# Query projections on 64 rows each, token splits read from PSUM, and MLP products placed among the last attention turns

## The chip, the core and the metric

The kernel runs on one core of a Trainium2 chip. The metric is the device time of one execution in microseconds. Engines are named as in the profile: PE is TensorE, PEld its weight loads, DVE is VectorE, ACT is ScalarE, POOL is GpSimd and SP is SyncE. PSUM has eight banks of 512 fp32 columns over 128 partitions.

## The reference

Linear attention with a positive feature map over 4 batches, 8 heads, 576 tokens and head size 64, then two MLPs of width 2048 on 2304 tokens of 512 features.

```python
def phi(x):
    proj = np.einsum('bhsd,df->bhsf', x, w_phi)
    proj = proj - np.max(np.abs(proj), axis=-1, keepdims=True)
    return np.concatenate([np.exp(proj), np.exp(-proj)], axis=-1)
q_p, k_p = phi(q), phi(k)
kv = np.einsum('bhsf,bhsd->bhfd', k_p, v);  z = np.sum(k_p, axis=2)
x = einsum(q_p, kv) / (einsum(q_p, z) + 1e-6)      # tokens x 512
h = x @ w1_in;  g = max(0.01 * h, h);          x = g @ w1_out
h = x @ w2_in;  g = h * tanh(softplus(h));     out = g @ w2_out
```

## The kernel before

**Precision.** A matmul whose operands are marked F32R is one pass of a shortened format. To keep accuracy each operand is split into a high part (an ACT copy) and a low part (a DVE subtraction), `split` at lines 79 to 81, and each product is three matmuls, `three` at lines 83 to 86: high by high, high by low, low by high. Plain fp32 matmuls (the attention's sums) go to the array as two instructions each, so that the trace counts 64 where the program writes 32.

**Attention.** The work goes by pairs of heads: 16 pairs, four to a batch. `attention(n)`, line 515, is one turn for n from 0 to 16. It works on five pairs at once: it loads n+3, transposes pair n+2, projects pair n+1 (`q_proj`, `k_proj`), takes the exponentials and the key-value sums of pair n (`k_exp`, `kv`, `kv_copy`), the output sums of pair n-1 (`nd`), and normalises pair n-2 and transposes it to features by tokens (`normalise`, `x_left`, `x_t`). Nothing reorders this: every engine runs its instructions in the order in which the code issues them. An odd n has one more key group to project and guard (`k_proj_left`); an even n has one more transpose to split.

**Query projection before.** A transposed query tile has 128 partitions: rows 0 to 63 are the features of an even token, rows 64 to 127 those of an odd one. The weights `wbh`, `wbl` are block diagonal (`wbd`, lines 253 to 258): the 128 columns of half `o` are zero in the rows of the other half. `q_proj(i, c)`, line 391, runs for c = 0 to 3 (head h, half o): three matmuls on all 128 rows with 256 or 320 columns into one bank of the ring "a" (four banks), then an ACT copy of the bank to `qd` (line 403). After both halves of a head, POOL takes the maximum over partitions (line 408), and `q_guard` (line 412, DVE) subtracts it.

**Weight conversion beside it.** The weights of the MLPs arrive as 64-bit words and are converted on DVE and ACT, one piece in each turn from 1 to 15 (`conv0`): lines 134 and 136 at the turn's begin, an ACT scale (150), and two DVE steps (159, 162) near its end. The ten first pieces are split in the following turn: ACT line 215, then DVE line 216, ahead of `normalise` in DVE's order.

**Tokens to MLP.** `x_t` ends with two ACT copies into `X`: 64 left-over columns (line 485, from the bank that `nd` writes, `outs`) and 512 columns from the bank `xt` (line 487). `window(0, (p,))`, called after turns 8 to 11 (line 781), splits one 128-row piece of batch 0's tokens from `X` into the MLP's operands, lines 80 and 81. `moe(0)` and `moe(1)` stand at the ends of turns 15 and 16. Each emits one product of the first MLP (`emit_h`, 12 matmuls of 512 columns) and its activation (`leaky`). After the turns the last `x_t(15)` follows, the attention's banks (`outs`, `kvp`, `xt`) are released and become the ring "b", and `moe(2)`, `moe(3)`, ... run the MLPs: each emits a product h and, two steps later, the output product of an earlier one.

Of the kernel before, what the change touches and what calls it, by code (L numbers as in the profile page):

```python
# [23 lines left out]
def attention_two_mlps_kernel(  # L24
# [12 lines left out]
    nc = tc.nc  # L37
# [38 lines left out]
    def bank(ring):  # L76
        return rings[ring].tile([P, 512], F32, tag=ring, name=ring)

    def split(hi, lo, src):
        nc.scalar.activation(out=hi, in_=src, func=AF.Copy)  # L80
        nc.vector.tensor_tensor(out=lo, in0=src, in1=hi.bitcast(F32), op=ALU.subtract)

    def three(o, wh_, wl_, xh, xl, start=True, stop=True):
        nc.tensor.matmul(out=o, lhsT=wh_, rhs=xh, start=start, stop=False)  # L84
        nc.tensor.matmul(out=o, lhsT=wh_, rhs=xl, start=False, stop=False)  # L85
        nc.tensor.matmul(out=o, lhsT=wl_, rhs=xh, start=False, stop=stop)  # L86
# [164 lines left out]
    with tc.manual_schedule():  # L251
# [136 lines left out]
            nc.scalar.activation(out=e, in_=src, func=AF.Exp, scale=float(sg))  # L388
            return e

        def q_proj(i, c):
            s = st[i]
            h, o = divmod(c, 2)
            if "qd" not in s:
                s["qd"] = ap.tile([P, 2, S], F32, tag="qd", name="qd")
                s["qm"] = ap.tile([P, 2, S], F32, tag="qm", name="qm", bufs=1)
            t = bank("a")
            n = HM + (h == o) * LEFT
            c0 = h * (HM + (1 - o) * LEFT)
            d0 = (1 - o) * (HM + h * LEFT)  # L400
            f = slice(o * F, (o + 1) * F)
            three(t[:, 0:n], wbh[:, f], wbl[:, f], s["qh"][:, c0:c0 + n], s["ql"][:, c0:c0 + n])
            nc.scalar.activation(out=s["qd"][:, h, d0:d0 + n], in_=t[:, 0:n], func=AF.Copy)  # L403
            half = s.setdefault("half", set())
            half.add(c)
            if {2 * h, 2 * h + 1} <= half:
                qd, qm = s["qd"][:, h, :], s["qm"][:, h, :]
                nc.gpsimd.partition_all_reduce(qm, qd, P, bass_isa.ReduceOp.absmax)  # L408

        def q_guard(i):  # L410
            s = st[i]
# [65 lines left out]
        def x_t(i):  # L477
            s = st[i]
            b, p = divmod(i, NP)
            t = pa.tile([P, 512], F32, tag="xt", name="xt")  # L480
            for j in range(NM):
                nc.tensor.transpose(out=t[:, j * P:(j + 1) * P], in_=s["xn"][:, j].rearrange("p h d -> p (h d)"), identity=ident)
            o = s["nd"][:, 1, MAIN - LEFT:MAIN]
            nc.tensor.matmul(out=o, lhsT=s["xl"].rearrange("p h d -> p (h d)"), rhs=fold, start=True, stop=True)
            nc.scalar.activation(out=X[:, p, C0 + b * LEFT:C0 + (b + 1) * LEFT], in_=o, func=AF.Copy)
            st[i] = None
            return lambda: nc.scalar.activation(out=X[:, p, b * MAIN:(b + 1) * MAIN], in_=t, func=AF.Copy)

        def k_exp(i, a):
# [5 lines left out]
        def start():  # L495

            transposes(0, "k")
            split(wbh, wbl, wbd.rearrange("p a f -> p (a f)"))
            transposes(0, "q")
            k_proj(0, 0)  # L500
            transposes(0, "l")
            q_left(0)
            q_proj(0, 1)
            q_proj(0, 2)
            k_proj(0, 1)
            q_proj(0, 0)
            q_proj(0, 3)
            k_proj_left(0)
            transposes(1, "q", "k")
            q_left(1)  # L510
            q_guard(0)
            load(2)
            conv0.load(1)

        def attention(n):

            x, o, w, p, t = (i if 0 <= i < PAIRS else None for i in range(n - 2, n + 3))
            x_copy = lambda: None  # L520
            if n + 3 < PAIRS:
                load(n + 3)
            if t is not None and t > 1:
                values(t)
            if n >= CONV0:
                conv0.begin()
                conv0.split()
            if p is not None:
                for c in range(4):
                    q_proj(p, c)  # L530
            if x is not None and n < PAIRS:
                normalise(x)
                x_left(x)
            if p is not None:
                for c in range(2):
                    k_proj(p, c)
                if p % 2 == 0:
                    k_proj_left(p)
            if w is not None:
                k_exp(w, 0)  # L540
            if x is not None:
                x_copy = x_t(x)
            if t is not None:
                transposes(t)
                q_left(t)
            if w is not None:
                k_exp(w, 1)
            x_copy()
            conv0.scale()
            if o is not None:  # L550
                nd(o)
            if p is not None:
                q_guard(p)
            conv0.join()
            if w is not None:
                st[w]["qp"] = [exp(st[w]["qd"], "qp", sg) for sg in (1, -1)]
                for a in range(2):
                    kv(w, a)
                kv_copy(w)
            if p is None:  # L560
                normalise(o)
                x_left(o)
            if p is None:
                moe(n - PAIRS + 1)

        order = [(0, MAIN), (MAIN, MAIN), (C0, B * LEFT)] + [(j * MAIN, MAIN) for j in range(2, B)]
        blocks = [(a, c0, n) for a in range(2) for c0, n in order]
        NB = len(blocks)
        win = {}

        def window(j, chunks=range(KD)):
            a, c0, n = blocks[j]
            for kk in chunks:
                hi = winp.tile([P, MAIN], F32R, tag="wh", name="wh")[:, 0:n]
                lo = winp.tile([P, MAIN], F32R, tag="wl", name="wl")[:, 0:n]
                split(hi, lo, X[:, kk, c0:c0 + n])
                win.setdefault(j, []).append((hi, lo))


# [138 lines left out]
        def moe(g):  # L718
            for x in [g, g + 1] if g == jump else [g + 1] if g > jump else [g]:
                if x < len(seq):  # L720
                    emit_h(seq[x])
                    if seq[x][1][-1] == M - 1 and seq[x][0] + 1 < NB:
                        window(seq[x][0] + 1)
            if g < len(seq):
                j, ms = seq[g]
                if j <= last1:
                    between = leaky(seq[g])
                    if j == 0 and ms[0] >= HEAD:
                        conv1.step(*between)
                        if not conv1.done():  # L730
                            conv1.step()
                        if conv1.at == len(conv1.units):
                            conv2.load(1)
                    else:
                        for f in between:
                            f()
            if 0 <= g - 2 < len(seq) and seq[g - 2][0] <= last1:
                j, ms = seq[g - 2]
                emit_o(seq[g - 2])
                if ms[-1] == M - 1:  # L740
                    for d in range(KD):
                        finish(j, d)
                if 0 < j < last1:
                    conv2.step()
                    if conv2.done() and not w_st:
                        load_w2(0)
                if j == last1:
                    m = ms[0]
                    split_w2(m, (0, 1) if m < M - 1 else (0,))
                    if m < M - 1:  # L750
                        load_w2(m + 1, (0, 1) if m < M - 2 else (0,))
                    else:
                        load_w2(m, (1,))
                        tail[0] = g + 1
            if g == tail[0]:
                split_w2(M - 1, (1,))
            done = None
            if 0 <= g - 3 < len(seq) and seq[g - 3][0] > last1:
                j, ms = seq[g - 3]
                if seq[g - 3] == seq[-1]:  # L760

                    emit_o(seq[-1], (0, 1))
                    finish(j, 0)
                    finish(j, 1)
                    for d in (2, 3):
                        for it in seq[-2:]:
                            emit_o(it, (d,))
                        finish(j, d)
                elif seq[g - 3] == seq[-2]:
                    emit_o(seq[-2], (0, 1))  # L770
                else:
                    emit_o(seq[g - 3])
                    if ms[-1] == M - 1:
                        done = j
            mish(g, done)

        start()
        for n in range(PAIRS + 1):
            attention(n)
            if 0 <= n - PAIRS // 2 < KD:  # L780
                window(0, (n - PAIRS // 2,))
        x_t(PAIRS - 1)()
        ap.release()
        pa.release()
# [44 lines left out]
```

## Time and profile before

| what | value |
|---|---|
| median of 3 runs | 981.86 us (980.54 to 982.08) |
| profiled execution | 982.12 us, of which the span of its instructions is 980.0 us |
| PE busy | 957.1 us (98%), mean granted clock 0.996 |
| DVE busy | 715.9 us (73%) |
| ACT busy | 507.2 us (52%) |
| POOL busy | 69.0 us (7%) |

The busy shares are means over two stages: some 190 us of attention, and the MLPs after them. The slices of the page show PE at 8 or 9 tenths in the attention and at 9 in nearly all that follows; DVE is at 8 and 9 in the attention. Which wait ends last has to be read in each stage for itself.

### The profile page before, as it was taken

Reading aid. Unit: us, or ns where it says so; the run is one execution under the profiler, and the core shown is the slowest. Engines: PE = TensorE matmul, PEld = TensorE weight load, DVE = VectorE, ACT = ScalarE, POOL = GpSimd, SP = SyncE. Lnnn points to the kernel's source line nnn. Section 1 sums busy time; section 2 is a strip of 40 time slices with the busy share of each in tenths; the row PEclk is TensorE's granted clock in tenths of the full one; section 3 lists DMA queues with packets and bytes.
Section 4 is the critical chain, followed back from the end, with each engine's and each line's share of the span. In section 5 each row is a group of like instructions: output and inputs, shape, how many; then the busy total and the mean of one; then the engine's idle time right before and its main releaser. Section 6 shows DMA issues by size and latency. Waiting matters only on the chain.

```text
span 980.0 us, 16741 instructions
## 1 busy us (share of the span) xinstructions
PE 957.1 (98%) x6704; PEld 818.4 (84%) x6704; DVE 715.9 (73%) x1271; ACT 507.2 (52%) x886; POOL 69.0 (7%) x36
## 2 busy tenths in 40 slices
PE   7999889899999999999999999999999999999998
PEld 7999778788888889988888888888888988888886
DVE  7899889389936665765334459878977788778875
ACT  5899879555523333333333456445545455445543
POOL 3443434000000000000000000000000000000000
PEclk9999999999999999999999999999999999999999
DMA  7444543235404444442203310001000100001001
GB/s 200 123 130 136 141 112 108 77 115 161 134 22 143 148 142 148 131 147 100 76 1 112 104 55 11 1 1 43 1 1 1 43 1 23 1 0 43 1 1 43
DMA packets 68205, 72.97 MB, mean 74 GB/s; under 512 B 27168, under 2 KB 52640, under 8 KB 68128
## 3 DMA queue, kind: packets, MB, share of 16 engines
q1 hardware_dynamic: 67392, 71.52, 23.8%
q8 instruction: 52, 0.85, 0.4%
q10 hardware_dynamic: 736, 0.39, 0.1%
q14 instruction: 25, 0.20, 0.1%
HBM read 57.48 MB, written 14.42 MB: 73 GB/s over the span
## 4 chain that ended last, share of the span: by engine, by line
PE 83%; DVE 7%; ACT 7%; issue 1%; DMA 0%; POOL 0%; POOLq 0%; ACTq 0%; DVEq 0%
PE a L84 14%; PE a L85 14%; PE a L86 14%; PE b L86 13%; PE b L85 13%; PE b L84 13%; ACT kp L388 2%; ACT qp L388 1%; DVE wl L216 1%; DVE xn L464 1%; DVE mx L365 1%; PE outs L448 1%; DVE qd L412 1%; DVE kd L366 1%; ACT xleft L474 1%
## 5 line engine op out<-in xcount | busy, mean ns | idle before, releaser
L84 PE MATMUL a<-wh,wh 128*128 128x512 f32 (+1 forms) x640 | 235.7, 368 | 0.0
L86 PE MATMUL a<-wh,wl 128*128 128x512 f32 (+1 forms) x640 | 235.4, 368 | 0.0
L85 PE MATMUL a<-wl,wh 128*128 128x512 f32 (+1 forms) x640 | 235.4, 368 | 0.0
L84 PEld LDWEIGHTS a<-wh,wh 128*128 128x128 f32 x640 | 120.6, 188 | 20.4 <-issue 0.2
L85 PEld LDWEIGHTS a<-wl,wh 128*128 128x128 f32 x640 | 120.7, 189 | 20.3
L86 PEld LDWEIGHTS a<-wh,wl 128*128 128x128 f32 x640 | 120.6, 188 | 19.9
L661 DVE TENSOR_TENSOR gl<-g,gh 128x512 fp32r<-128x512 f32 x72 | 49.8, 692 | 110.2 <-ACT gh L658 110.2
L85 PE MATMUL b<-gl,wh 128*128 128x512 f32 (+1 forms) x320 | 117.7, 368 | 0.0
L84 PE MATMUL b<-gh,wh 128*128 128x512 f32 (+1 forms) x320 | 117.7, 368 | 0.0
L86 PE MATMUL b<-gh,wl 128*128 128x512 f32 (+1 forms) x320 | 117.7, 368 | 0.0
L86 PE MATMUL b<-wh,gl 128*128 128x512 f32 x288 | 112.2, 390 | 0.0
L85 PE MATMUL b<-wl,gh 128*128 128x512 f32 x288 | 112.2, 389 | 0.0
L84 PE MATMUL b<-wh,gh 128*128 128x512 f32 x288 | 112.1, 389 | 0.0
L658 ACT ACTIVATE gh<-g 128x512 fp32r<-128x512 f32 x72 | 45.5, 632 | 116.0 <-PE b L86 110.7
L683 ACT ACTIVATE gh<-u 128x512 fp32r<-128x512 f32 x72 | 45.5, 633 | 70.3 <-PE b L85 63.6
L657 DVE TENSOR_TENSOR g<-g,a 128x512 f32<-128x512 f32 x72 | 49.4, 686 | 41.1 <-ACT g L654 38.4
L408 POOL PARTITION_ALL_REDUCE qm<-qd x32 | 68.8, 2197 | 100.7 <-ACT qd L403 94.0
L710 ACT ACTIVATE r<-e,two 128x512 f32<-128x512 f32 x72 | 51.7, 718 | 36.5 <-DVE e L695 36.5
L84 PEld LDWEIGHTS b<-gh,wh 128*128 128x128 f32 x320 | 60.4, 189 | 10.1
L86 PEld LDWEIGHTS b<-gh,wl 128*128 128x128 f32 x320 | 60.3, 189 | 10.0
L85 PEld LDWEIGHTS b<-gl,wh 128*128 128x128 f32 x320 | 60.3, 188 | 9.9
L679 ACT ACTIVATE e<-a 128x512 f32<-128x512 f32 x72 | 43.0, 597 | 47.8 <-PE a L86 26.8
(116 smaller groups left out, 1638.2 us busy)
## 6 DMA issues: line engine op xcount, KB each, us to landing
stage<-in_moe_w_in_dram SPq DMA_DIRECT2D x32, 512.0 KB, 3.8
stage<-in_moe_w_out_dram SPq DMA_DIRECT2D x32, 512.0 KB, 3.6
scr<-c SPq DMA_DIRECT2D x37, 256.0 KB, 2.0
wstage<-scr SPq DMA_DIRECT2D x32, 256.0 KB, 3.7
qn<-in_q_dram SPq DMA_DIRECT2D x16, 256.0 KB, 4.6
vmain<-in_v_dram SPq DMA_DIRECT2D x32, 128.0 KB, 3.4
kn<-in_k_dram SPq DMA_DIRECT2D x15, 256.0 KB, 4.4
out_dram<-X SPq DMA_DIRECT2D x15, 256.0 KB, 2.1
```

Of the source, the lines that this page charges most:

```text
L84: nc.tensor.matmul(out=o, lhsT=wh_, rhs=xh, start=start, stop=False)
L85: nc.tensor.matmul(out=o, lhsT=wh_, rhs=xl, start=False, stop=False)
L86: nc.tensor.matmul(out=o, lhsT=wl_, rhs=xh, start=False, stop=stop)
L216: return lambda: nc.vector.tensor_tensor(out=lo, in0=src, in1=hi.bitcast(F32), op=ALU.subtract)
L388: nc.scalar.activation(out=e, in_=src, func=AF.Exp, scale=float(sg))
L408: nc.gpsimd.partition_all_reduce(qm, qd, P, bass_isa.ReduceOp.absmax)
L657: nc.vector.tensor_tensor(out=g, in0=g, in1=h, op=ALU.max)
L658: nc.scalar.activation(out=hi, in_=g, func=AF.Copy)
L661: nc.vector.tensor_tensor(out=lo, in0=g, in1=hi.bitcast(F32), op=ALU.subtract)
L679: nc.scalar.activation(out=e0, in_=h0, func=AF.Exp)
L683: nc.scalar.activation(out=hi2, in_=u2, func=AF.Copy)
L710: nc.scalar.activation(out=r0, in_=e0, func=AF.Ln, bias=two)
```

## The change

1. `q_proj(i, h)` does both halves of a head at once. It takes two banks, and its six matmuls read only the 64 rows of their half (`HALVES[o]`), of weights and tokens alike, alternating between the halves. Two ACT copies and one POOL maximum follow, as before.
2. In `x_t` the left-over columns go to the bank `kvp` of the following pair, columns 448 to 511, in place of the same columns of `outs`.
3. For batch 0, `x_t` returns `window(0, (p,), t)`: the split of the 512 columns straight from the bank `xt`, without a copy in `X`. It runs in turns 2 to 5, where `x_copy()` stands. The calls after turns 8 to 11 are gone.
4. The second exponential of the keys, `k_exp(w, 1)`, comes earlier in turn 0 and turn 15. `moe(0)` moves into turn 15, ahead of `x_t(13)`; `moe(1)` to the end of turn 15; the product of `moe(2)` ahead of `x_t(15)`. In `start` the projections of pair 0 stand after its second `k_proj`, and pair 1's query transposes ahead of `k_proj_left`.

```diff
-        def q_proj(i, c):
+        def q_proj(i, h):
...
+            ts = [bank("a") for _ in range(2)]
+            at = []
+            for o in range(2):
+                n = HM + (h == o) * LEFT
+                c0 = h * (HM + (1 - o) * LEFT)
+                at.append((ts[o][:, 0:n], HALVES[o], slice(o * F, (o + 1) * F), slice(c0, c0 + n)))
+            for j, (w, x) in enumerate(((wbh, s["qh"]), (wbh, s["ql"]), (wbl, s["qh"]))):
+                for t, r, f, c in at:
+                    nc.tensor.matmul(out=t, lhsT=w[r, f], rhs=x[r, c], start=(j == 0), stop=(j == 2))
...
-            o = s["nd"][:, 1, MAIN - LEFT:MAIN]
+            o = st[min(i + 1, PAIRS - 1)]["kvp"][:, MAIN - LEFT:MAIN]
...
+            if b == 0:
+                return lambda: window(0, (p,), t)
...
             if w is not None:
                 k_exp(w, 0)
+            if n == 0:
+                k_exp(w, 1)
+            if n == PAIRS - 1:
+                k_exp(w, 1)
+                moe(0)
             if x is not None:
                 x_copy = x_t(x)
...
-            if p is None:
-                moe(n - PAIRS + 1)
+            if n == PAIRS - 1:
+                moe(1)
...
-        def window(j, chunks=range(KD)):
+        def window(j, chunks=range(KD), src=None):
...
-                split(hi, lo, X[:, kk, c0:c0 + n])
+                split(hi, lo, X[:, kk, c0:c0 + n] if src is None else src)
...
         for n in range(PAIRS + 1):
             attention(n)
-            if 0 <= n - PAIRS // 2 < KD:
-                window(0, (n - PAIRS // 2,))
+        emit_h(seq[HEAD])
         x_t(PAIRS - 1)()
```

Where the order moves, first on DVE in turn 2. `qth` and `qtl` are the two parts of the transposed queries, `qd` the guarded projections, `e` and `c` a piece of converted weights, `wl` the low part of tokens (from `xt`) or of weights (from `c`). Before:

```order
L361 CAST qth<-lh 128x64
L361 CAST qtl<-ll 128x64
L412 TENSOR_TENSOR qd<-qd,qm 128x1152
L159 SCALAR_TENSOR_TENSOR e<-stage 128x512
L162 SCALAR_TENSOR_TENSOR c<-c,e 128x512
```

The change:

```order
L361 CAST qth<-lh 128x64
L361 CAST qtl<-ll 128x64
L81 TENSOR_TENSOR wl<-xt,wh 128x512
L414 TENSOR_TENSOR qd<-qd,qm 128x1152
L159 SCALAR_TENSOR_TENSOR e<-stage 128x512
L162 SCALAR_TENSOR_TENSOR c<-c,e 128x512
```

One subtraction has come in ahead of the guard; it reads the ACT copy that now stands where the copy of `xt` to `X` stood.

Second, ACT in turn 15, from the scaling of `xleft` of pair 13 on. `kp` are exponentials of keys, `qp` of queries, `g` and `gh` belong to `leaky(0)`, `X` from `outs`, `kvp` or `xt` are the token copies. Before:

```order
L474 ACTIVATE xleft_86<-outs,den 64x64 x2
L388 ACTIVATE kp<-kd 128x1024
L485 ACTIVATE X<-outs 128x64
L388 ACTIVATE kp<-kd 128x1024
L487 ACTIVATE X<-xt 128x512
L150 ACTIVATE c<-c 128x512
L388 ACTIVATE qp<-qd 128x1152 x2
L434 ACTIVATE kv<-kvp 128x260
```

The change:

```order
L476 ACTIVATE xleft_86<-outs,den 64x64 x2
L388 ACTIVATE kp<-kd 128x1024 x2
L663 ACTIVATE g<-a 128x512
L667 ACTIVATE gh<-g 128x512
L487 ACTIVATE X<-kvp 128x64
L492 ACTIVATE X<-xt 128x512
L150 ACTIVATE c<-c 128x512
L388 ACTIVATE qp<-qd 128x1152 x2
L436 ACTIVATE kv<-kvp 128x260
```

The two exponentials are now neighbours, and the first MLP product's activation stands ahead of the token copies.

Third, PE from the key-value sums of pair 14 on (`kvp`), with the first three of each product's twelve matmuls. Before:

```order
L428 MATMUL kvp<-vleft_107,lp 64x2x65 x2
L482 MATMUL xt<-ident,xn 128x128 x4
L484 MATMUL outs<-fold,xleft_86 128x64
L448 MATMUL outs<-kv,qp 64x65 x32
L453 MATMUL outs<-kv,qp 64x65 x4
```

The change:

```order
L430 MATMUL kvp<-vleft_107,lp 64x2x65 x2
L84 MATMUL a<-wh,wh_597 128x512
L85 MATMUL a<-wl,wh_597 128x512
L86 MATMUL a<-wh,wl_598 128x512
...
L484 MATMUL xt<-ident,xn 128x128 x4
L486 MATMUL kvp<-fold,xleft_86 128x64
L450 MATMUL outs<-kv,qp 64x65 x32
L455 MATMUL outs<-kv,qp 64x65 x4
```

The first product stands between the sums and the transposes of pair 13, and the left-over columns go to another bank than the one that line 450 writes next.

## Rows read from the trace of the kernel before

**Rows 1.** Windows: stretch, us; busy PE, PEld, DVE, ACT, POOL; granted clock, DMA, GB/s.
```profile
49.00:73.50 24.50, 24.05 (x490) 22.36 (x490) 22.95 (x46) 22.89 (x45) 10.26 (x5) 1.00 0.46 130
122.50:147.00 24.50, 20.51 (x369) 18.50 (x369) 22.00 (x39) 19.26 (x38) 8.81 (x4) 1.00 0.42 112
176.50:180.20 3.70, 3.70 (x72) 3.70 (x74) 0.69 (x1) 1.90 (x3) 0.00 (x0) 0.54 0.08 27
196.00:220.50 24.50, 24.50 (x110) 20.29 (x109) 20.34 (x38) 12.76 (x22) 0.00 (x0) 1.00 0.34 115
```
**Rows 2.** Timeline of ACT: line 434 in turns 6 to 12 (start, duration, instruction).
```profile
85.71 0.41 ACT L434 ACTIVATE kv<-kvp 128x260 f32<-128x260 f32 x1
95.31 0.40 ACT L434 ACTIVATE kv<-kvp 128x260 f32<-128x260 f32 x1
106.14 0.41 ACT L434 ACTIVATE kv<-kvp 128x260 f32<-128x260 f32 x1
118.11 0.40 ACT L434 ACTIVATE kv<-kvp 128x260 f32<-128x260 f32 x1
130.98 0.41 ACT L434 ACTIVATE kv<-kvp 128x260 f32<-128x260 f32 x1
142.95 0.41 ACT L434 ACTIVATE kv<-kvp 128x260 f32<-128x260 f32 x1
155.21 0.41 ACT L434 ACTIVATE kv<-kvp 128x260 f32<-128x260 f32 x1
```
**Rows 3.** Timeline of DVE, turns 2 and 3; in brackets idle time and its releaser.
```profile
41.64 1.35 DVE L412 TENSOR_TENSOR qd<-qd,qm 128x1152 f32<-128x1152 f32 x1
...
45.82 0.69 DVE L216 TENSOR_TENSOR wl<-c,wh 128x512 fp32r<-128x512 f32 x1 [0.75 <-ACT wh L215]
...
52.31 1.35 DVE L412 TENSOR_TENSOR qd<-qd,qm 128x1152 f32<-128x1152 f32 x1
```
**Rows 4.** Timeline of ACT, turns 2, 3 and 12.
```profile
41.75 0.62 ACT L487 ACTIVATE X<-xt 128x512 f32<-128x512 f32 x1
...
51.36 0.61 ACT L487 ACTIVATE X<-xt 128x512 f32<-128x512 f32 x1
...
55.09 0.64 ACT L215 ACTIVATE wh<-c 128x512 fp32r<-128x512 f32 x1 [0.23 <-DVE c L162]
...
147.47 0.63 ACT L474 ACTIVATE xleft<-outs,den 64x64 f32<-64x64 f32 x2 [2.39 <-DVE xn L464]
```
**Rows 5.** Timeline of DVE, beginning of turn 9.
```profile
107.10 0.69 DVE L81 TENSOR_TENSOR wl<-X,wh 128x512 fp32r<-128x512 f32 x1 [1.43 <-ACT wh L80]
...
108.38 1.78 DVE L216 TENSOR_TENSOR wl<-c,wh 128x512 fp32r<-128x512 f32 x1
```
**Rows 6.** Groups by form, 0 to 245 us: a subtraction that reads PSUM (busy, mean ns).
```profile
L81 DVE TENSOR_TENSOR qtl<-a,qth 128x512 fp32r<-128x512 f32 x16 | 10.9, 684 | 1.2 <-ACT qth L80 1.1
```
**Rows 7.** Timeline of PE, turn 9: first and last query matmul, first of the keys.
```profile
105.28 0.41 PE L84 MATMUL a<-qth,wbh 128*128 128x320 f32 x1
...
106.84 0.31 PE L86 MATMUL a<-qth,wbl 128*128 128x320 f32 x1
...
107.97 0.39 PE L84 MATMUL a<-wbh,kth 128*128 128x256 f32 x1 [0.82 <-ACT qd L403]
```
**Rows 8.** Timeline of PE, turns 14 to 16.
```profile
168.68 2.09 PE L448 MATMUL outs<-kv,qp 128*64 128x65 f32 x64 [0.73 <-ACT X L485]
...
174.59 0.63 PE L482 MATMUL xt<-ident,xn 128*128 128x128 f32 x4 [1.27 <-DVE xn L464]
...
176.50 3.66 PE L448 MATMUL outs<-kv,qp 128*64 128x65 f32 x64 [0.90 <-ACT X L485]
...
187.85 2.09 PE L448 MATMUL outs<-kv,qp 128*64 128x65 f32 x64 [1.57 <-ACT X L485]
```
**Rows 9.** Timeline, turns 0 and 1: ACT, then DVE.
```profile
20.35 0.60 ACT L80 ACTIVATE qth<-a 128x512 fp32r<-128x512 f32 x1 [1.28 <-issue]
...
26.94 0.69 DVE L365 TENSOR_REDUCE mx<-a 128x4 f32<-128x512 f32 x1 [1.87 <-PE a L86]
```

More of the change, by code (lines that the diff above doesn't have):

```diff
@@ L389, in exp @@
             return e
-        def q_proj(i, c):
+        def q_proj(i, h):
             s = st[i]
-            h, o = divmod(c, 2)
             if "qd" not in s:
@@ L396, in q_proj @@
                 s["qm"] = ap.tile([P, 2, S], F32, tag="qm", name="qm", bufs=1)
[L397 to L408, printed above, removed]
+            ts = [bank("a") for _ in range(2)]
[7 more added lines that the diff above has]
+                    nc.tensor.matmul(out=t, lhsT=w[r, f], rhs=x[r, c], start=(j == 0), stop=(j == 2))
+            for o, (t, r, f, c) in enumerate(at):
+                d0 = (1 - o) * (HM + h * LEFT)
+                nc.scalar.activation(out=s["qd"][:, h, d0:d0 + c.stop - c.start], in_=t, func=AF.Copy)
+            qd, qm = s["qd"][:, h, :], s["qm"][:, h, :]
+            nc.gpsimd.partition_all_reduce(qm, qd, P, bass_isa.ReduceOp.absmax)
         def q_guard(i):
@@ L482, in x_t @@
                 nc.tensor.transpose(out=t[:, j * P:(j + 1) * P], in_=s["xn"][:, j].rearrange("p h d -> p (h d)"), identity=ident)
-            o = s["nd"][:, 1, MAIN - LEFT:MAIN]
+            o = st[min(i + 1, PAIRS - 1)]["kvp"][:, MAIN - LEFT:MAIN]
             nc.tensor.matmul(out=o, lhsT=s["xl"].rearrange("p h d -> p (h d)"), rhs=fold, start=True, stop=True)
             nc.scalar.activation(out=X[:, p, C0 + b * LEFT:C0 + (b + 1) * LEFT], in_=o, func=AF.Copy)
-            st[i] = None
+            if i < PAIRS - 1:
+                st[i] = None
+            if b == 0:
+                return lambda: window(0, (p,), t)
             return lambda: nc.scalar.activation(out=X[:, p, b * MAIN:(b + 1) * MAIN], in_=t, func=AF.Copy)
@@ L502, in start @@
             q_left(0)
-            q_proj(0, 1)
-            q_proj(0, 2)
             k_proj(0, 1)
             q_proj(0, 0)
-            q_proj(0, 3)
+            q_proj(0, 1)
+            transposes(1, "q")
+            q_left(1)
             k_proj_left(0)
-            transposes(1, "q", "k")
-            q_left(1)
+            transposes(1, "k")
             q_guard(0)
@@ L528, in attention @@
             if p is not None:
-                for c in range(4):
-                    q_proj(p, c)
+                for h in range(2):
+                    q_proj(p, h)
             if x is not None and n < PAIRS:
@@ L545, in attention @@
                 q_left(t)
-            if w is not None:
+            if w is not None and 0 < n < PAIRS - 1:
                 k_exp(w, 1)
@@ L720, in moe @@
                 if x < len(seq):
-                    emit_h(seq[x])
+                    if x != HEAD:
+                        emit_h(seq[x])
                     if seq[x][1][-1] == M - 1 and seq[x][0] + 1 < NB:
```

## The prediction

> **What bounds the kernel now.** I first read the busy time by stretches. From 196 us to the end PE is full at the full clock: 24.50 us of 24.50, 110 matmuls of 512 columns, 0.223 us each [rows 1]. So the MLPs neither shrink nor wait, and the change can only move the moment at which PE becomes full, less the MLP products that it has done by then. Before it, the attention's turns have no single bound. In an ordinary stretch PE, DVE and ACT are all near full (24.05, 22.95, 22.89 us of 24.50), and in the stretch of turns 10 and 11 none is (20.51, 22.00, 19.26) [rows 1]. Engines that are all busy and none full hand work to and fro, so I next read the waits inside one turn. In turn 2 DVE stands 0.75 us before line 216 for ACT's line 215 [rows 3]; in turn 3 ACT stands 0.23 us before line 215 for DVE's line 162 [rows 4]. Two turns are thus one run through DVE and one through ACT, and PE ends none of their waits. Third, I took each turn's length from the copies at line 434, one a turn: 9.60 us for an odd turn and 10.83 for an even one (turns 7 and 8), then 11.97, 12.87, 11.97 and 12.26 for turns 9 to 12 [rows 2]. Those four come after the four calls of `window`. Last I read PE's own gaps at the end of the attention [rows 8], because there PE is what the MLPs wait for.
>
> **A, the start.** In turn 0 ACT stands 1.28 us before the copy of `qth`; in turn 1 DVE stands 1.87 us for PE's key projections [rows 9]. The change puts the second exponentials of keys into the first gap: the row after them in ACT's order, the query exponentials, and with them the copies that free the banks for those key projections, come up to 1.28 us sooner. Against it, the projections of pair 1 now take two banks at once, one of which is freed only by the last subtraction of its keys, some 0.3 us later than now (estimated from one 0.684 us subtraction [rows 6], of which half is hidden). I take -1.0; the bounds are 0 (the gap is filled by something else) and -1.9 (DVE's whole wait goes).
>
> **B, the split moved into turns 2 to 5.** On ACT it replaces a copy of the same size, at no cost. On DVE one subtraction comes in ahead of the guard; none such from `xt` is in the trace, and its nearest row, also out of PSUM, is 0.684 us [rows 6]. In an even turn it waits for the ACT copy, which ends at 42.37 (41.75 + 0.62) [rows 4], so the guard that starts at 41.64 [rows 3] starts at some 43.05, 1.4 later. The 0.75 us that DVE stands idle before line 216 [rows 3] absorbs about half, which leaves 0.65. In an odd turn the copy ends at 51.97, before the guard's 52.31, so there is no wait, but no slack either, because ACT already waits for line 162 [rows 3, 4]: 0.68. Two of each: +2.7. Behind the new wait stand the guard and lines 159 and 162 of DVE, and for 162 ACT's line 215. Bounds: +1.4 (odd turns alone) and +5.6 (1.4 each).
>
> **C, the calls after turns 8 to 11 gone.** Turns 9 to 11 should take what turns 7 and 8 take: 11.97 - 9.60, 12.87 - 10.83 and 11.97 - 9.60 make 2.37 + 2.04 + 2.37 = 6.8 [rows 2]. One sees what goes: DVE stands 1.43 us for the ACT half of the split, does 0.69, and line 216 behind it takes 1.78 us in place of 0.69 [rows 3, 5]. Turn 12 has no line 215 or 216, so it is no ordinary even turn. It gets back between 12.26 - 10.83 = 1.43 and the 2.39 us that ACT stands before line 474 [rows 2, 4]; I take 2.0. Sum -8.8, bounds -8.2 and -9.2. No engine is late next: turns 6 to 8 are the proof of what such a turn costs.
>
> **D, the end of the attention.** From 168 us PE's gaps are 0.73, 1.27, 0.90 and 1.57 us, and line 448 at 176.50 took 3.66 us in place of 2.09 [rows 8], because the granted clock was 0.54 there, near the lower level of 1.2 GHz [rows 1]: another 1.57. That makes 6.04. Three of the gaps (0.73, 0.90, 1.57) are waits of line 448 for the copy of the left-over columns out of `outs`; with those columns in `kvp` it has nothing to wait for. The gap of 1.27 and the slow clock behind it go because the first product, 12 x 0.223 = 2.7 us, stands there. The second product fills the place behind the last `kvp` sums, and the third covers the last normalisation. New is one wait: in today's order the third product covers the last two ACT copies before the banks become the ring "b"; now nothing does. That costs the 0.61 of such a copy [rows 4], a small copy, and the hand-over, an estimated 0.95 in all. Net -5.1. ACT has to follow: `leaky(0)` puts its two instructions and a wait for DVE, some 1.9 us from rows of that size [rows 4, 6], ahead of the last query exponentials. PE needs these only after two more blocks of work of 2.7 us or less, so I let them hide. Bounds: -2.5 (ACT is late by the size of one product) and -6.0 (the new wait hides as well).
>
> **E, the query projections.** In turn 9 they take 105.28 to 107.15, 1.87 us, and then PE stands 0.82 us for the copies to free a bank [rows 7]. In turns 2 to 13 whatever PE saves lengthens that wait, so it is worth nothing there. It counts at the start, where A is bounded by the copies anyway, and once in turn 14, ahead of D. The trace has no matmul on 64 rows. The nearest rows alternate between the array's halves of columns: 64 instructions of 65 columns in 2.09 us, 0.50 ns for each column [rows 8]. The full-array query matmuls need the same: 3136 columns from the first start to the last in 1.56 us [rows 7]. So halves of columns show no overlap, and I take 0 for halves of rows, with 0.9 (half of 1.87) as the other bound. The Trainium skill speaks for the other bound: "TensorEngine Tiling (Array Packing)", sections Theoretical Speedup and Key Properties, has two tiles of 64 rows work in parallel, up to twice as fast, but says that a change of tiling mode drains the engine. By that page the sum would be up to 0.9 us lower; no row here shows it.
>
> **Sum.** -1.0 + 2.7 - 8.8 - 5.1 + 0 = -12.2. Against the profiled execution's own 982.12 us (span 980.0, and 2.1 around it) this gives 969.9. The median of the three runs is 0.26 below that execution, which I leave in the range.
>
> **Rivals.**
> 1. The halves of rows do overlap. For it: different rows, different banks, no shared operand. Against it: the halves of columns [rows 8]. Turn 14 gains 0.9 and the start a little: 968.9.
> 2. The split in turns 2 to 5 costs more: DVE is late by its whole 1.4 in all four turns, or line 216 falls behind POOL's start and stretches to 1.78 [rows 5]. Against it: line 216 keeps its place right behind ACT's line 215. Four times 1.1 more: 974.3.
> 3. ACT becomes the bound of turns 15 and 16, since the product's activation stands ahead of the copies and query exponentials. PE waits before the last two runs of line 448; D shrinks to -2.5: 972.5.
> 4. The change doesn't do what it says at the end: PE's banks or operands make the products wait, and D and A are near zero: 976.0. With B at its bound as well it would be within 0.2%.
> 5. Slower: the clock. PE does the same turns with less work between its waits, and in the one place of the end where it had little to do, the granted clock fell to 0.54 and line 448 took 1.75 times as long [rows 1, 8]. If that came in ordinary turns, PE's 10 us of a turn (24.05 of 24.50 over 2.4 turns) would become some 16, 6 more than the turn has. Two such turns eat the gain; with four it is 969.9 + 24 = 994. Against it: in the stretch of turns 10 and 11 PE was busy for only 20.51 of 24.50 us and the clock stayed at 1.00 [rows 1], and an ordinary turn less 0.9 is fuller than that. The Trainium skill has this rule against gaps in "TensorE: Matmul & The Clock Gate", section Why this matters for your kernels: a PE left idle between bursts of matmuls falls back to half its clock. The row of 176.50 agrees; that of turns 10 and 11 shows that gaps of that size don't suffice.
>
> **How the numbers follow.** Forecast 0.50, rival 1 0.20, rival 2 0.12, rival 3 0.09, rival 4 0.04, rival 5 0.05. The likeliest is 969.9. The range takes in the forecast with its bounds and rivals 1 to 3: from 967.0 (A, D and E all near their far ends, less what is unlikely to coincide) to 975.5 (rival 2 with a smaller D). A measurement of this kernel can tell about 0.2%, 2 us, from no change. All cases but 5 and half of 4 are faster by more than that: 0.93 faster, 0.02 the same, 0.05 slower.
>
> **What would show it.** In the trace after: copies of line 434 (now 436) some 9.6 and 10.8 us apart in turns 6 to 11 (C); turns 2 to 5 longer by 0.65 each (B); DVE's first wait of turn 1 shorter by 1 us (A); no PE wait at the line of the output sums, no clock of 0.54 after turn 13, and one wait of about 1 us ahead of the first `b` matmul (D); six pairs of query matmuls in 1.9 us, or in 0.9 for rival 1 (E). The prediction is wrong if turns 9 to 12 stay near 12 us, if the granted clock falls in the turns, or if PE waits for ACT in turns 15 and 16 for more than 2 us.

## The result, and the profile after

| | before | after |
|---|---|---|
| median of 4 runs | 981.2 us (980.42 to 982.08) | 972.43 us (971.68 to 974.28) |
| profiled execution, its span | 982.12, 980.0 us | 971.68, 969.7 us |
| first `b` matmul in that span | 196.38 us | 186.04 us |
| mean granted clock | 0.996 | 0.996 |

The ratio is 0.9913, with a 95% interval of 0.9896 to 0.9931: the changed kernel is 0.9% faster. The profiled execution before is the slowest of its four and the one after is the fastest of its four, so that the traces differ by 10.3 us where the medians differ by 8.8. Of the 10.3 us between the two spans, 10.34 lie ahead of the first `b` matmul; from there to the end they take 783.6 and 783.7 us. So the MLPs did not change, as the prediction has it, and everything is found between the copies of `kv` (line 434, now 436). ACT's timeline after shows them from turn 0 to turn 12, some rows cut (start, duration, instruction), where [rows 2] show them for turns 6 to 12:

```profile
24.29 0.40 ACT L436 ACTIVATE kv<-kvp 128x260 f32<-128x260 f32 x1
...
44.20 0.40 ACT L436 ACTIVATE kv<-kvp 128x260 f32<-128x260 f32 x1
54.44 0.40 ACT L436 ACTIVATE kv<-kvp 128x260 f32<-128x260 f32 x1
65.86 0.41 ACT L436 ACTIVATE kv<-kvp 128x260 f32<-128x260 f32 x1
77.59 0.39 ACT L436 ACTIVATE kv<-kvp 128x260 f32<-128x260 f32 x1
88.65 0.40 ACT L436 ACTIVATE kv<-kvp 128x260 f32<-128x260 f32 x1
98.25 0.40 ACT L436 ACTIVATE kv<-kvp 128x260 f32<-128x260 f32 x1
109.08 0.41 ACT L436 ACTIVATE kv<-kvp 128x260 f32<-128x260 f32 x1
...
149.23 0.41 ACT L436 ACTIVATE kv<-kvp 128x260 f32<-128x260 f32 x1
```

The stretches between such copies, in us ("to 3" runs from the copy of turn 2 to that of turn 3; "tail" from the last copy to the first `b` matmul), make a ledger that sums to the 10.34:

| stretch | before | after | difference |
|---|---|---|---|
| up to copy 0 | 24.95 | 24.29 | -0.66 |
| to 1, 2 | 8.89, 11.02 | 8.91, 11.00 | 0.00 |
| to 3, 4 | 9.60, 10.83 | 10.24, 11.42 | +1.23 |
| to 5, 6 | 9.60, 10.82 | 11.73, 11.06 | +2.37 |
| to 7, 8 | 9.60, 10.83 | 9.60, 10.83 | 0.00 |
| to 9, 10, 11, 12 | 11.97, 12.87, 11.97, 12.26 | 9.61, 10.82, 9.61, 10.11 | -8.92 |
| to 13, 14, 15 | 9.00, 9.22, 9.39 | 8.99, 8.68, 9.37 | -0.57 |
| tail | 13.56 | 9.77 | -3.79 |

Two rows are not as forecast: the stretch to 5, and the end. First the stretch to 5. PE's timeline after, turn 5 (in brackets the idle time and its releaser), then windows of the same place (stretch; busy PE, PEld, DVE, ACT, POOL; granted clock, DMA, GB/s):

```profile
67.80 0.39 PE L84 MATMUL a<-wbh,kth 128*128 128x256 f32 x1 [1.92 <-ACT qd L408]
...
68.74 0.36 PE L85 MATMUL a<-wbl,kth 128*128 128x256 f32 x1
68.89 0.42 PE L86 MATMUL a<-wbh,ktl 128*128 128x256 f32 x1
```
```profile
66.00:68.00 2.00, 0.20 (x1) 0.20 (x2) 1.91 (x4) 1.48 (x5) 0.00 (x0) 1.00 0.46 123
68.00:70.00 2.00, 2.00 (x14) 2.00 (x14) 1.90 (x6) 1.35 (x6) 1.89 (x1) 0.70 1.03 369
70.00:72.00 2.00, 2.00 (x12) 2.00 (x12) 1.97 (x4) 1.15 (x2) 2.00 (x2) 0.50 0.59 142
72.00:74.00 2.00, 2.00 (x45) 1.83 (x46) 1.45 (x4) 1.50 (x4) 0.37 (x1) 0.95 0.47 104
```

PE waits 1.92 us for ACT to empty a bank of queries, begins the key projections at full speed, and 0.94 us later its matmuls lengthen from 0.28 to 0.42 us: the granted clock goes to 0.70 and 0.50, the lower of its two levels (1.2 GHz), and is back by 74. The Trainium skill, "TensorE: Matmul & The Clock Gate", section Why this matters for your kernels, says that a PE left idle between bursts of matmuls falls back to half its clock. The fall behind this wait agrees with that; the wait of 1.91 us in turn 3 (at 46.14), behind which the clock stayed at 1.00, does not.

Now the end. PE's timeline after, turns 15 and 16, where [rows 8] showed four waits; then ACT's around the first of the two that are left:

```profile
169.70 2.09 PE L450 MATMUL outs<-kv,qp 128*64 128x65 f32 x64
...
173.32 1.16 PE L427 MATMUL kvp<-vmain,kp 128*64 128x65 f32 x32 [1.30 <-ACT X L487]
...
179.35 2.08 PE L450 MATMUL outs<-kv,qp 128*64 128x65 f32 x64
...
186.04 0.50 PE L84 MATMUL b<-gh,wh 128*128 128x512 f32 x1 [0.80 <-ACT X L492]
```
```profile
169.15 2.01 ACT L388 ACTIVATE kp<-kd 128x1024 f32<-128x1024 f32 x2
171.18 0.60 ACT L663 ACTIVATE g<-a 128x512 f32<-128x512 f32 x1
172.53 0.63 ACT L667 ACTIVATE gh<-g 128x512 fp32r<-128x512 f32 x1 [0.75 <-DVE g L666]
173.06 0.20 ACT L487 ACTIVATE X<-kvp 128x64 f32<-128x64 f32 x1
```

The waits at the output sums (line 450) are gone, those sums take 2.09 us, and a new wait of 1.30 us stands ahead of the last key-value sums: their bank `kvp` still holds pair 13's left-over columns, whose copy (line 487) stands on ACT behind the activation of the first MLP product.

Last, the query projections. PE's timeline after, first and last row of one block of twelve matmuls, and the key projections behind it:

```profile
24.04 0.41 PE L405 MATMUL a<-qth,wbh 64*128 64x320 f32 x2
...
24.80 0.31 PE L405 MATMUL a<-qth,wbl 64*128 64x320 f32 x2
25.36 0.39 PE L84 MATMUL a<-wbh,kth 128*128 128x256 f32 x1 [0.25 <-ACT qd L408]
```

From 24.04 to 25.11 (24.80 + 0.31) the block takes 1.07 us, where the full array needs 1.87 [rows 7]. Two halves of rows do work at once here; the Trainium skill's "TensorEngine Tiling (Array Packing)", section Theoretical Speedup, is borne out by 1.75 of its factor of two.

### The profile page after: what moved, and what is told of

It reads as the page before. It is cut to its first block, busy times and chain, and to the rows that moved or that the text cites. A ratio compares the mean times of both kernels' runs of the same rounds, so it can differ in the third digit from the quotient of the medians.

```text
span 969.7 us, 16741 instructions
## 1 busy us (share of the span) xinstructions
PE 944.9 (97%) x6704; PEld 807.3 (83%) x6704; DVE 712.3 (73%) x1271; ACT 504.7 (52%) x882; POOL 68.4 (7%) x36
## 4 chain that ended last, share of the span: by engine, by line
PE 84%; DVE 9%; ACT 6%; issue 1%; DMA 0%; POOL 0%; POOLq 0%; ACTq 0%; DVEq 0%
PE a L84 14%; PE a L85 14%; PE a L86 14%; PE b L84 14%; PE b L86 14%; PE b L85 14%; ACT kp L388 1%; DVE qd L414 1%; DVE mx L365 1%; DVE kd L366 1%; ACT qp L388 1%; DVE xn L466 1%; DVE wl L216 1%; DVE e L159 1%; DVE c L162 1%
```

## The experiments

Each was timed beside the kernel before on one chip: combo_halves on another chip than the rest, so that its ratio compares better than its median. The theory after these traces: the gain is C and D; B costs its 0.6 a turn; what the halves of rows save goes into PE's wait, worth nothing, and the longer wait lets the clock fall. The rivals: the overlap is itself worth something, the fall has another cause, or the new wait at the end is hidden anyway.

| kernel | median, us | ratio to before, 95% interval |
|---|---|---|
| full_rows | 971.68 | 0.9898 (0.9883 to 0.9913) |
| early_left | 970.19 | 0.9892 (0.9877 to 0.9906) |
| halves_only | 980.93 | 0.9999 (0.9991 to 1.0008) |
| window_only | 973.66 | 0.9929 (0.9915 to 0.9943) |
| filler | 970.83 | 0.9895 (0.9879 to 0.9911) |
| tail_only | 978.56 | 0.9967 (0.9956 to 0.9979) |
| late_low | 970.24 | 0.9887 (0.9873 to 0.9901) |
| combo | 966.84 | 0.9853 (0.9839 to 0.9867) |
| combo_halves | 967.05 | 0.9864 (0.9847 to 0.9880) |

**full_rows**: the change with its query projections back on all 128 rows.

```diff
-                at.append((ts[o][:, 0:n], HALVES[o], slice(o * F, (o + 1) * F), slice(c0, c0 + n)))
+                at.append((ts[o][:, 0:n], slice(0, P), slice(o * F, (o + 1) * F), slice(c0, c0 + n)))
```

> The changed kernel with the query matmuls on all 128 rows again, order and banks unchanged. Theory: turn 5 was 2.1 us longer than before the change, and only 0.7 of that is the moved split; the rest is the granted clock, which fell from 68.7 to 72.2 us after PE had stood 1.92 us for a bank, a gap made longer by the faster query projections. With full rows the gap shrinks by 0.8 us, the clock stays at 1.00, turn 5 takes some 10.3 us, and the span is about 969.0 (1.4 back, 0.7 lost at the start and in turn 14). Rival: the moved split itself costs turn 5 its 2.1 us (DVE late); then turn 5 stays at 11.7 and the span is about 970.4.

PE's timeline and the windows in turn 5 of this kernel:

```profile
66.60 0.38 PE L84 MATMUL a<-wbh,kth 128*128 128x256 f32 x1 [1.10 <-ACT qd L408]
```
```profile
66.00:68.00 2.00, 1.40 (x11) 1.41 (x12) 1.91 (x6) 1.42 (x5) 1.09 (x1) 1.00 0.69 267
68.00:70.00 2.00, 2.00 (x20) 1.89 (x18) 1.93 (x4) 1.91 (x5) 2.00 (x2) 1.00 0.97 290
```

The wait is 1.10 in place of 1.92, the clock stays at 1.00, and the stretches to 3, 4, 5, 6 are 10.24, 11.41, 10.24, 11.42. So the stretch to 5 lost 1.49 to the clock, of which the stretch to 6 gave back 0.36. The stretches to 2 and from 7 to 14 are as in the changed kernel; the one to 14, where the overlap should have counted, is 8.69 against 8.68. The stretch to 15 is 9.61 against 9.37, so there the halves are worth 0.24 against the same order on full rows; tail_only (below), with the projections of before, has 9.38 as well.

The start went against the expectation. Full rows were to lose there, yet copy 0 comes at 23.40 in place of 24.29, and the clock does not fall ahead of it. This kernel and combo, the two traces with full rows and the new order of the start, have copy 0 at 23.40 and 23.42 and a clock of 1.00 there; the five with 64 rows have it at 24.25 to 25.67, with a fall in every one. That the 64 rows bring on the fall at the start is thus a rival that no run separates from chance: the clock also fell there on full rows in the old order, in two traces of three. The medians of the two kernels, 971.68 and 972.43, are too near to tell apart.

**filler**: the change with four matmuls of 512 columns more in turns 3 and 5, ahead of the key projections, into a tile that nothing reads. The halves of rows stay.

```diff
+                if n in (3, 5):
+                    d = pa.tile([P, 512], F32, tag="xt", name="fill")
+                    for _ in range(4):
+                        nc.tensor.matmul(out=d, lhsT=wbh[:, 0:P], rhs=st[p]["kh"][:, 0:512], start=True, stop=True)
```

> The changed kernel with four matmuls of 512 columns, which nothing reads, put into PE's two longest gaps (turns 3 and 5, ahead of the key projections; 1.92 us each). Theory: the granted clock fell in turn 5 because PE stood still there, not because the rows are halved; with the gap filled for some 0.9 us the clock stays at 1.00, turn 5 takes 10.24 us as with full rows, and the span is 1.1 below the changed kernel's (968.6 with its clock at the start). Rival: matmuls on 64 rows themselves count as little work, so the clock falls all the same: turn 5 at 11.7.

PE's timeline in turn 5, then the windows:

```profile
65.80 1.20 PE L538 MATMUL fill<-kth,wbh 128*128 128x512 f32 x4
67.78 0.39 PE L84 MATMUL a<-wbh,kth 128*128 128x256 f32 x1 [0.78 <-ACT qd L408]
```
```profile
66.00:68.00 2.00, 1.22 (x5) 0.70 (x5) 1.93 (x4) 1.48 (x5) 0.00 (x0) 1.00 0.35 111
68.00:70.00 2.00, 2.00 (x19) 2.00 (x19) 1.90 (x6) 1.35 (x6) 1.91 (x1) 1.00 0.96 350
```

The key projections start at the same moment as in the changed kernel (67.78, 67.80), but the clock holds, and the stretches to 5 and 6 are 10.24 and 11.43. More work for PE, and a shorter turn: this speaks for PE's idleness, and against the form of the matmuls, as what the fall follows. Nothing else in the order moved. Still, it is one trace without the fall against two with it (the changed kernel and early_left), and the wait in turn 3 had no fall in either of those.

**halves_only** and **window_only**: the kernel before with one part of the change each: the new `q_proj` (part 1, its core shown, with the order of pair 0's projections at the start that goes with it), and the split moved into turns 2 to 5 (the first line of the second diff is in `x_t`; the calls after turns 8 to 11 go).

```diff
+                at.append((ts[o][:, 0:n], HALVES[o], slice(o * F, (o + 1) * F), slice(c0, c0 + n)))
```

> The kernel before with the 64-row query projections alone (with the order of pair 0's projections that they need at the start). Theory: six pairs take 1.07 us in place of 1.87, PE stands that much longer for a bank in turns 2 to 13, turn 14 and the start gain 0.5: span 979.5 if the clock holds. Where PE's gap grows to about 1.9 us (turns 9 to 12 had the longest gaps) the clock falls, at some 1.5 us each: up to 985. Rival: gaps of that size don't lower the clock: 979.5 and 1.00 in all turns.

```diff
+            if b == 0:
+                return lambda: window(0, (p,), t)
...
-            if 0 <= n - PAIRS // 2 < KD:
-                window(0, (n - PAIRS // 2,))
```

> The kernel before with the moved split alone: batch 0's tokens split from their bank in turns 2 to 5, no calls after turns 8 to 11. Theory: turns 2 to 5 cost 0.65 each (+2.6), turns 9 to 12 give 8.9 back, the clock stays at 1.00 since the query projections fill PE as before: span 973.7, turn 5 about 10.3 us. Rival: turn 5's 2.1 us are the split's own: span 975.2, turn 5 about 11.7 us.

The halves alone are worth 0.01% (interval 0.9991 to 1.0008). Every stretch from 2 on is as before within 0.03, with PE's waits ahead of the keys longer, up to 1.63 us in the stretch to 11, and the clock at 1.00 in the turns. The moved split alone gives 7.3 us by the medians: +0.64, +0.59, +0.64, +0.60 in the stretches to 3 to 6, and 9.61, 10.83, 9.62, 10.10 in those to 9 to 12. It carries most of the 8.8. One row of its trace was not expected: PE's waits at the end are those of before [rows 8], but the clock did not fall between them. PE's timeline of window_only, turns 15 and 16:

```profile
167.49 0.63 PE L482 MATMUL xt<-ident,xn 128*128 128x128 f32 x4 [1.27 <-DVE xn L464]
...
169.40 2.09 PE L448 MATMUL outs<-kv,qp 128*64 128x65 f32 x64 [0.90 <-ACT X L485]
...
179.16 2.09 PE L448 MATMUL outs<-kv,qp 128*64 128x65 f32 x64 [1.57 <-ACT X L485]
```

The same waits and 2.09 us in place of 3.66: the stretch to 15 is 7.82 against 9.39. In halves_only, with such waits too (1.26, 0.90, 1.58), the same sums took 3.18 and the clock fell. So equal orders at the end get unequal clocks from one trace to another.

**tail_only**: the kernel before with the end of the attention as in the change: the left-over columns in `kvp`, `moe(0)` and `moe(1)` in turn 15, the third product ahead of `x_t(15)`.

```diff
-            o = s["nd"][:, 1, MAIN - LEFT:MAIN]
+            o = st[min(i + 1, PAIRS - 1)]["kvp"][:, MAIN - LEFT:MAIN]
...
+            if n == PAIRS - 1:
+                k_exp(w, 1)
+                moe(0)
```

> The kernel before with part 4 at the end (second exponential, the three products' places) and the left-over columns in the next pair's bank alone. Theory: the time from the last key-value copy but one to the first output product falls by what the changed kernel shows, about 4 us: turn 15 and the stretch after it take 9.4 + 9.8 us in place of 9.4 + 13.6, with a wait of 1.3 us before the key-value sums of pair 15; turns 1 to 13 stay; span about 975.5. Rival: the gain at the end is mostly the granted clock, which fell there before and may stay up by chance; then the span is about 978.

It gives 3.3 us by the medians. The stretches to 14, 15 and the tail are 8.69, 9.38 and 9.76, those of the changed kernel; the new wait ahead of the last key-value sums is there (1.01 us), and the 0.80 ahead of `b` too. The end is a gain of its own, independent of the turns. The two gains, 7.3 and 3.3, add up to 10.6 by the medians, 1.8 more than the changed kernel has; the fall in turn 5 accounts for 1.1 of that, and the rest is open.

**early_left**: the change with the first product's activation behind the token copies of pair 13 on ACT.

```diff
-                moe(0)
+                emit_h(seq[0])
...
                 x_copy = x_t(x)
+            if n == PAIRS - 1:
+                for f in leaky(seq[0]):
+                    f()
```

> The changed kernel with the left-over columns of pair 13 copied out of their bank ahead of the first MLP product's activation in turn 15. Theory: the wait of 1.30 us before the key-value sums of pair 15 is a wait for that copy and nothing else, so it goes, and the MLPs start 1.3 us earlier: span 968.4. Rival: ACT is the bound of turn 15 (query exponentials end at 176.3), so the wait turns up again before the last output sums: span 969.5.

ACT's timeline in turn 15, then PE's:

```profile
170.50 2.01 ACT L388 ACTIVATE kp<-kd 128x1024 f32<-128x1024 f32 x2
172.53 0.22 ACT L487 ACTIVATE X<-kvp 128x64 f32<-128x64 f32 x1
172.65 0.59 ACT L666 ACTIVATE g<-a 128x512 f32<-128x512 f32 x1
```
```profile
171.05 2.08 PE L450 MATMUL outs<-kv,qp 128*64 128x65 f32 x64
...
173.20 1.10 PE L427 MATMUL kvp<-vmain,kp 128*64 128x65 f32 x32
```

The copy now stands right behind the exponentials, the wait of 1.30 is gone, and the tail is 8.21 in place of 9.77. The wait was real time, and its cause is the order on ACT. The span is 969.6 all the same, as in this trace the clock fell for longer at the start (copy 0 at 25.67). In turn 5 the wait of 1.91 and the fall of the clock are as in the changed kernel (stretch to 5: 11.76), as they should be, since nothing there was touched.

**late_low**: the change with the DVE half of the moved split issued behind line 162, in place of ahead of the guard.

```diff
-                return lambda: window(0, (p,), t)
+                return lambda: window(0, (p,), t, lows)
...
+            while lows:
+                lows.pop()()
```

> The changed kernel with the DVE half of the moved split issued behind the second conversion step of the turn, in place of ahead of the guard. Theory: in even turns DVE's wait of 0.67 us for the ACT half goes, and the subtraction falls into the 0.75 us that DVE has there: turns 2 and 4 are back at 11.0 and 10.83 with nothing later in the next; odd turns keep 0.6; PE's gaps after even turns shrink from 1.92 to about 1.3 and the clock stays at 1.00. Span 1.2 us less for the split and 1.1 for the clock: about 967.4. Rival: the cost of the split in even turns is its length, not its place: turns 3 to 6 as in the changed kernel.

The split's cost fell from 2.47 (the four stretches of window_only) to 1.0: the stretches to 3, 4, 5, 6 are 9.63, 11.31, 9.61, 11.29. Counted by the copies that end the stretches, the free places are 3 and 5, and I had expected them at the even turns; counted by the turn that issues the split they are turns 2 and 4, since a split issued in turn 2 stands just ahead of that turn's copy and delays what comes after it. DVE's timeline of late_low shows why those are free:

```profile
45.01 0.68 DVE L593 TENSOR_TENSOR wl<-xt,wh 128x512 fp32r<-128x512 f32 x1
...
46.53 0.69 DVE L216 TENSOR_TENSOR wl<-c,wh 128x512 fp32r<-128x512 f32 x1 [0.17 <-ACT wh L215]
```

Of DVE's wait of 0.75 before line 216 in turn 2 [rows 3], 0.17 is left; the split sits in the rest. In turns 3 and 5 there is no such wait. PE's waits ahead of the keys fell with it, to 1.29 and 1.27, and the clock did not fall in the turns. The span is 968.5 against an expected 967.4: again the clock fell for longer at the start (copy 0 at 25.66).

**combo** and **combo_halves**: late_low and early_left together, with the third product split around `x_t(15)`; the first with projections on all 128 rows, the second with 64.

```diff
-        emit_h(seq[HEAD])
-        x_t(PAIRS - 1)()
+        emit_h(seq[HEAD], (0, 1))
+        last = x_t(PAIRS - 1)
+        emit_h(seq[HEAD], (2, 3))
+        last()
```

> The changed kernel with full rows, the early copy of the left-over columns, the DVE half of the split behind the conversion step, and the third product cut in two, half ahead of the last transposes and half behind them. Theory: against full rows alone (span 967.7, clock 1.00) 1.3 us from the wait before the sums of pair 15, 0.8 from the wait for the released banks, 1.2 from the split's place: span about 964.4, median about 966.5. Rival: the gains overlap because ACT becomes the bound at the end: 966.

> The combination with the query projections on 64 rows each, so that this one edit separates it from the combination (966.84 us, first b matmul at 180.48, turns 9.63, 11.33, 9.61, 11.32, 9.61). It asks whether the overlap of the halves is worth anything once PE's waits in turns 2 to 6 are short. Theory (the attention's turns are set by the run through DVE and ACT, so PE's 0.8 us a turn are worth nothing there): the six pairs take 1.07 us, PE's wait ahead of the key projections grows to some 1.3 us in turns 2 to 6 and to at most 1.65 in turns 6 to 12, the clock stays at 1.00 in the turns, and the turns are as in the combination within 0.1 us; the time is 966.8 within 1.5 us. Rival a (the overlap is worth something where PE leads): turns 13 and 14 or the start are shorter by 0.8 us each, 965.2. Rival b (the clock still falls with the 64 rows): a turn of 2 to 6 lengthens by a microsecond or more and its window shows a granted clock of 0.7 or less, 968 or above.

PE's timeline of combo, from the second half of the third product to the first `b` matmul:

```profile
178.18 0.60 PE L484 MATMUL xt<-ident,xn 128*128 128x128 f32 x4
178.77 0.43 PE L486 MATMUL kvp<-fold,xleft 128*128 128x64 f32 x2
179.01 0.48 PE L84 MATMUL a<-wh,wh 128*128 128x512 f32 x1
...
180.48 0.39 PE L84 MATMUL b<-gh,wh 128*128 128x512 f32 x1
```

The six matmuls from 179.01 on cover the two ACT copies, and no wait is left ahead of `b`: the tail is 7.62, and the kernel, at 0.9853 of before, beats both. With 64 rows the same kernel is at 0.9864, and the intervals overlap: PE's waits in turns 3 and 5 grow from 0.48 and 0.50 to 1.28 and 1.27, the clock stays at 1.00 there, and the stretches to 3 up to 14 agree within 0.04. The 0.8 us that PE saves in each of these turns is worth nothing; as before, the stretch to 15 is shorter by 0.24 (9.39 against 9.63), and copy 0 comes 0.83 later, behind a fall of the clock.

## Why the prediction was right, and where it was not

The forecast of 969.9 us is 2.5 below the median of 972.43 and 1.8 below the profiled execution; its range (967.0 to 975.5) holds both. The gain was forecast as 12.2 us and is 10.4 between the profiled executions and 8.8 between the medians. C and the price of B came as worked out. Of the 1.9 us missing between the traces, the clock in turn 5 took 1.1 and a wait that D overlooked took 1.3; smaller differences go the other way. And 1.57 of the forecast gain is the clock's fall at the end of one trace [rows 8], of the slowest of before's executions; window_only, where it did not come, shows that it is not a fixed cost of that order. That the range also held the medians, which moved less, is in part luck. By its own steps:

**A** (forecast -1.0): -0.66 in this trace, but the start varies by as much between traces. The clock falls for some microseconds between 15 and 23 us in some traces, in before's too, and not in others; and the three traces with before's own start have copy 0 at 24.95, 24.28 and 24.16 (before, window_only, tail_only). Between two traces at 1.00 it is -0.88 (window_only 24.28, full_rows 23.40), between two with a fall -1.07 (halves_only 25.36, the changed kernel 24.29). These agree with the forecast, but don't prove its size. What holds in every trace is DVE's wait, the second of these rows:

```profile
20.94 0.60 ACT L80 ACTIVATE qth<-a 128x512 fp32r<-128x512 f32 x1 [0.47 <-PE a L341]
```
```profile
26.37 0.69 DVE L365 TENSOR_REDUCE mx<-a 128x4 f32<-128x512 f32 x1 [1.03 <-PE a L86]
```

ACT's 1.28 and DVE's 1.87 [rows 9] have shrunk to 0.47 and 1.03. DVE's wait is 1.67 to 1.99 in the four traces with the second exponentials in their old place, and 0.74 to 1.23 in the seven with them in the new one.

**B** (+2.7): the split alone costs +2.47, by window_only. The even turn goes as worked out. DVE's timeline after, turns 2 and 3:

```profile
41.74 0.69 DVE L81 TENSOR_TENSOR wl<-xt,wh 128x512 fp32r<-128x512 f32 x1 [0.67 <-ACT wh L80]
42.35 1.35 DVE L414 TENSOR_TENSOR qd<-qd,qm 128x1152 f32<-128x1152 f32 x1
...
45.80 0.69 DVE L216 TENSOR_TENSOR wl<-c,wh 128x512 fp32r<-128x512 f32 x1
...
52.29 0.68 DVE L81 TENSOR_TENSOR wl<-xt,wh 128x512 fp32r<-128x512 f32 x1
```

The guard starts 1.85 us ahead of its turn's copy, where it started 3.22 ahead (44.86 by the ledger, less 41.64 [rows 3]): 1.37 later, forecast 1.4. The 0.75 before line 216 is gone, and in turn 3 there is no wait. What was missed is the 1.13 on top that the clock took in turn 5, which makes the four stretches +3.60.

**C** (-8.8): -8.92, each of the four stretches within 0.15 of its forecast. The stretch that [rows 1] give in their second line is near full again after, on all three engines, and line 216 at the beginning of turn 9 has its 0.69 us, not the 1.78 of [rows 5]:

```profile
122.50:147.00 24.50, 22.98 (x492) 21.59 (x494) 22.85 (x45) 23.10 (x46) 10.93 (x6) 1.00 0.54 150
```
```profile
110.04 0.69 DVE L216 TENSOR_TENSOR wl<-c,wh 128x512 fp32r<-128x512 f32 x1 [0.75 <-ACT wh L215]
```

**D** (-5.1): -4.35, from the stretches to 14, 15 and the tail. The four waits and the slow clock went, all 6.04, and the new wait before `b` is 0.80 (forecast 0.95). With the 1.30 that was not forecast this makes -3.94; where the last 0.41 comes from is open. The step that failed is "PE needs these only after two more blocks of work of 2.7 us or less, so I let them hide". It followed the query exponentials behind `leaky(0)` and forgot the copy of the left-over columns, which stands behind `leaky(0)` too. With those columns moved to `kvp`, the next sums in that bank wait for it: 1.30 us, by early_left worth 1.56. The change had moved a wait from one bank to another, and I looked only at the bank that was freed. Rival 3 had the cause (ACT late behind the first product's activation), though not the place or the size.

**E** (0): nearly right in what it is worth, wrong in its reason. The halves of rows do overlap (1.07 against 1.87), so rival 1 had the mechanism. The 0.9 in turn 14 that it built on it is not there (8.68 against 8.69 in the stretch to 14, and 0.24 in the one to 15). The reading behind the 0 was at fault too: "halves of columns show no overlap" set plain fp32 sums [rows 8] against F32R projections [rows 7]. The plain fp32 row on the full array is line 486; PE's timeline after, turn 3:

```profile
48.47 0.33 PE L486 MATMUL kvp<-fold,xleft 128*128 128x64 f32 x2
48.64 0.60 PE L341 MATMUL a<-ident,qn 128*128 128x128 f32 x4
```

Its two instructions of 64 columns take 0.17 us to the next start, 1.3 ns for each column, against the 0.50 of the halves. Two instructions are few, and loading of weights may be in it, but the row takes away the ground for "no overlap": whether halves of columns overlap is not shown here.

**The clock** (rival 5, 0.05): by the forecast's own sign ("if the granted clock falls in the turns") it was wrong here. The mechanism came once, for 1.13 us, where the rival counted some 6 a turn for as many as four turns. The argument against it used a mean (20.51 busy of 24.50); what went with the fall in turn 5 is one wait, 1.10 us in full_rows and 1.92 with the halves. Step E says that what PE saves lengthens that wait, and rival 1 has the halves save 0.9, but the two were never put together. Rival 2's time of 974.3 would have come from a split that costs more; the split did not. Rival 4's "within 0.2%" is a slip: with B at its bound its 976.0 becomes 978.9, 0.3% below before's 981.86.

**What stays open.** Why the clock fell after the wait of 1.92 us in turn 5 and not after that of 1.91 in turn 3, why it falls at the start of some traces and not of others, whether the 64 rows have a part in that, and so how much of the spread between runs of one kernel it makes (979.64 to 983.21 in 17 runs of the kernel before). By the medians the difference between the changed kernel (-8.8) and filler (-11.0) is larger than the 1.1 that the trace shows, but their intervals overlap.

## What to carry to other kernels

Two engines that hand work to and fro pay for each instruction in the place where neither waits, and nothing in the place where one does: the same split cost some 2.2 a call in turns 9 to 12, 0.6 in turns 2 to 5, and 0 behind line 162 of an even turn. When a tile is moved to another bank to end a wait, list who writes that bank next, and where its reader stands in its engine's order. Work saved on an engine that then waits is worth nothing, and a longer wait of PE may cost its clock. Before a row stands in for another, compare their formats: a price per column of plain fp32 says nothing about F32R.

## What the runs showed of the hardware

- Matmuls on 64 rows in the two halves of rows, with different banks, overlap: twelve in 1.07 us, against 1.87 on the full array.
- PE waited 1.91 to 1.92 us in turns 3 and 5 of the changed kernel and of early_left; in each the clock fell to 0.50 after the second and not after the first. After waits of 1.63 us and less in turns 1 to 13 of the other kernels it stayed at 1.00. With the wait of turn 5 cut to 0.78 by matmuls that nothing needs, it stayed at 1.00.
- At the start, a wait of PE that ends near 15 us was 1.74 to 2.52 us long. The clock fell behind it in eight traces of eleven; it did not after waits of 1.74, 1.76 and 2.52 us (full_rows, combo, window_only).
- With the same waits (1.27, 0.90, 1.57 us within 0.01), the clock fell at the end of before and of halves_only and not of window_only: 64 matmuls of 65 columns took 3.66, 3.18 and 2.09 us.
